# Windowed attention with a gated feed-forward: the RMS weight row by one broadcast transfer, its constant moved, first-block copies in halves, loads in a new order

## The chip, the cores and the metric

The kernel runs on one core of one Trainium2 chip. The core has a matrix engine (TensorE, PE in the profile, with its weight loads as PEld), a vector engine (VectorE, DVE), a scalar engine (ScalarE, ACT), a general engine (GpSimd, POOL), and a synchronising engine (SyncE, SP). SP, ACT and POOL issue DMA transfers. Each engine works through its own queue in order, and an instruction waits for its inputs by semaphores. The metric is the time of one execution on the device, in microseconds (us); lower is better.

## What is computed

Attention over a window of 128 positions and four sink positions, and a normalised gated feed-forward network on the result:

```python
# q, k, v: (4, 8, 768, 64) float32; n_sink 4, window 128
scores = q @ k^T / 8
keep = (pos_k < 4) | (0 <= pos_q - pos_k < 128)
a = softmax(where(keep, scores, -1e9)); x = a @ v        # -> (3072, 512)

rms = sqrt(mean(x * x, axis=-1) + 1e-06)
xn = x / rms * rms_g
g = xn @ w_gate                                         # (512, 1536)
silu = g / (1 + exp(-g))
out = (silu * (xn @ w_val)) @ w_out                     # (1536, 512)
```

## The kernel before

The 3072 tokens are 24 blocks of 128 (four batches of six blocks). For each block `g` the kernel loads q, k and v, transposes q and k (blocks 0 to 7 on PE with a copy out of PSUM, later ones by DMA), multiplies k by q of its own and the next block (`scores`, L445), takes the exponential on ACT (`exps`, L463), masks, and multiplies by v (`av`, L501). v has an extra column of ones for each head, so that the last column of the product is the denominator. On DVE `normal` (L526) divides by it. `square` (L537, on ACT) sums the squares of a row; `rms` (L545, on DVE) makes the reciprocal root by an integer first guess and a few small steps, and multiplies the block by it and by the weight row `gb`, into `xr`. `xr` is transposed on PE for blocks 0 to 8 (`pe_x`, L575), and copied out of PSUM (`copy_x`).

The feed-forward part works in groups `G` of four blocks. `ffn` (L832) does, for a set of 128-wide slices of the inner dimension (`fts`) and a set of columns, the gate matmuls (`g`), the value matmuls (`v`), the hyperbolic tangent on ACT (`tanh`), and two steps on DVE (`silu`, `hidden`). Group 0 is worked in four chunks of one block each (`CHUNKS`), four slices at a time, group 1 and 2 in two chunks. `project` multiplies by `w_out`, `evacuate` copies out, `store` writes.

The order of all of this is not written by hand. Every instruction is given to `Plan` (L27) with the engines that may run it, a duration, what it needs and gives, a priority and the PSUM banks that it takes and drops. `Plan.run` is a list scheduler: it repeatedly takes the operation that can start first, by its own durations, and the engines' queues are filled in that order. `Plan.land` says when it takes a transfer to be complete. So a changed duration, priority or load order can move instructions anywhere in the queues; at run time the queues are fixed and each instruction waits only for its real inputs.

Loads of q, k, v and the weights go through POOL's queue, float32 in memory to bfloat16 on chip, in the order of the string `LOADS`; at most `DEPTH` = 8 are outstanding. `w-0-2` stands for slices 0 and 1 of both `w_gate` and `w_val`. Block 0's k and q are loaded as float32 through SP (`F32_LOADS`) and cast on ACT. The weight row is loaded through SP as one row of 512 (`grow`, L341) between these two. `unit_gb` (L398) multiplies it by a column of ones in float32 on PE, which spreads it over the 128 partitions; `scale_gb` (L401, ACT) copies it out and multiplies it by `C3`, a constant of the reciprocal root.

The masks of blocks 0 and 1 are added before the scores by matmuls of a bias (`PE_MASKS` = 2, `mask_bias` L435, four matmuls for each block), those of blocks 2 to 15 are multiplications on DVE (`mask_dve` L475), and from block 16 on selections on POOL (`mask_pool`). The scores of blocks 0 and 1 are done in two parts (`SPLIT`), first for the block's own q and then for the next. `WARM` = 30 small matmuls on zeros fill gaps of PE early on.

```python
    LOADS = "q-1 k-1 v-0 w-0-2 v-1 qkv-2 qkv-3 w-2-4 w-4-6 w-6-8 w-8-9 w-9-12 qkv-4 wo-0-6 qkv-5 wo-6-12 qkv-6 qkv-8 qkv-7"
```

Of the kernel before, what the change touches and what calls it, by code (L numbers as in the profile page):

```python
# [9 lines left out]
ALU = mybir.AluOpType  # L10
# [5 lines left out]
P = 128  # L16
# [3 lines left out]
C3 = -5.0 / 16.0  # L20
# [6 lines left out]
class Plan:  # L27
# [5 lines left out]
    LATE = 300  # L33
    HOP = {"PE": 40, "ACT": 35, "DVE": 35, "POOL": 90, "SP": 60}
    START = {"PE": 800, "ACT": 800, "DVE": 1030, "POOL": 1290, "SP": 800}

    def __init__(self):
        self.ops, self.held = [], {}
        self.rings = {"POOL": 0, "HW": 0, "TR": 0}
        self.banks = {i: 0 for i in range(8)}  # L40
# [7 lines left out]

    def land(self, ring, first, work):


        r = self.rings
        if ring == "POOL":
            begin = max(first, r["POOL"], r["HW"])
            r["POOL"] = begin + (1.4 * work if begin < 8500 else work)
            self.loads -= 1
            return r["POOL"] + 520
        if ring == "HW":
            begin = max(first, r["HW"])
            r["HW"] = begin + (1.25 * work if begin > 2500 else work)  # L60
# [6 lines left out]
        return r["TR"] + (350 if ring == "TR" else 650)  # L67

    def run(self):
        free, users = dict(self.START), {}  # L70
        self.loads = sum(o["ring"] == "POOL" for o in self.ops)
# [10 lines left out]
        while left:  # L82
            first = None
            for e, found in cand.items():
                for o in found:
# [3 lines left out]
                    ready = o["ready"] + self.HOP[e] if o["ready"] else 0  # L89
                    if k:  # L90
                        ready = max(ready, sorted(self.banks.values())[k - 1] + 40)
                    start = max(free[e], ready)
                    key = (start, o["prio"], ready, o["at"])
# [6 lines left out]
            (start, *_), e, o = first  # L100
            for x in o["ways"]:
                cand[x].remove(o)
# [34 lines left out]
def kernel(  # L137
# [35 lines left out]
    CAST_DVE = 600  # L173
    MASKS_PRIO = -5
    POOL_AT = (1,2)
    DEPTH = 8
    LOADS = "q-1 k-1 v-0 w-0-2 v-1 qkv-2 qkv-3 w-2-4 w-4-6 w-6-8 w-8-9 w-9-12 qkv-4 wo-0-6 qkv-5 wo-6-12 qkv-6 qkv-8 qkv-7"
    LOADS += "".join(f" qkv-{g}" for g in range(9, NB))
    PE_MASKS = 2
    POOL_MASK_FROM = 16  # L180
# [3 lines left out]
    GATE_FROM = 6  # L184
    LOAD_LEAD = 9
    LEAD_FROM = 10
    WARM = 30
    GATE_LEAD = 6
    T_LEAD = 3
    SPLIT = (0,1)  # L190
    CHUNKS = (4,2,2)
    GB_PRIO = 2000
# [33 lines left out]
    ones = const.tile([1, P], FP32, name="ones")  # L226
    sel = const.tile([P, P], BF16, name="sel")
    headm = const.tile([P, H], FP32, name="headm")
    grow = const.tile([1, DM], FP32, name="grow")
# [22 lines left out]
    for b in range(B):  # L252
        dve(60, lambda b=b: nc.vector.memset(V16[b][:, :, :, D:VW], 1.0),
            gives=[("vone", b)], prio=-97 + b if b == 0 else -50)
    dve(150, lambda: nc.vector.memset(ones, 1.0), gives=["ones"], prio=-96)
# [77 lines left out]
    for i, name in enumerate(F32_LOADS):  # L333
# [8 lines left out]
        out=grow, in_=moe_rms_g.rearrange("(o d) -> o d", o=1)))}, (), ["grow"], -89.5,  # L342
        ring="HW", work=50)
    act(1290, None, (), ["table"], -80)

    issue = []
# [51 lines left out]
    def unit_gb():  # L398
# [520 lines left out]
```

The softmax here doesn't subtract the row's maximum and nothing guards it: scores larger than these inputs give would overflow.

## Time and profile before

| | |
|---|---|
| median of 8 runs | 247.02 us (246.54 to 247.48) |
| the profiled execution, own time | 246.54 us |
| its span, first to last instruction | 244.8 us |
| first feed-forward matmul starts | 20.16 us |
| PE / DVE / ACT / POOL busy | 234.1 / 183.3 / 131.1 / 88.7 us |
| PE matmuls recorded | 2098 |
| granted TensorE clock | 1.00 |

The profile is of one execution. Its page has busy times, the span in 40 slices, the chain of work that ended last, and the costliest groups of instructions; the trace behind it can be asked for the instructions of a stretch in order of time (the timeline), for busy times by stretch (the windows), and for who waited for whom. In a timeline line the first two numbers are the start and the duration in us, then come the engine, the line of the kernel, the operation, its tiles as output<-inputs, the shapes and the number of instructions that are drawn together; in brackets stands the idle time of the engine before it and what ended it. A line of the waits has what waited, for what, the sum in us, how often, and the longest.

### The profile page before, as it was taken

The page shows a single profiled execution, that of the slowest core. Times are in us where ns is not written, and L with a number is a line of the kernel's source. Part 1 is how long each engine was busy: PE and PEld are TensorE (multiplying, and loading weights), DVE is VectorE, ACT ScalarE, POOL GpSimd, SP SyncE. Part 2 cuts the span into 40 slices and gives each one's busy share as a digit, 9 for nine tenths or more (in the row PEclk, how much of TensorE's full clock was granted, in tenths as well). Part 3 has the DMA queues.
Part 4 walks back from the last instruction along what each step waited for, and adds up shares of the span by engine and source line. Part 5 has one row for each costly group of instructions (what it writes and reads, how often), then busy time and mean ns, then how long its engine had stood idle before and what let it go on. Part 6 is the DMA issues. An engine that isn't in the chain of part 4 may idle for free.

```text
span 244.8 us, 5510 instructions
## 1 busy us (share of the span) xinstructions
PE 234.1 (96%) x2098; PEld 148.8 (61%) x2120; DVE 183.3 (75%) x482; ACT 131.1 (54%) x276; POOL 88.7 (36%) x114
## 2 busy tenths in 40 slices
PE   4898999999999999999999999999999999999994
PEld 2477997776789775688874544444545544444443
DVE  4188979979899998899889499991299992377700
ACT  3577565778676647555627555735735521333111
POOL 8986755785354759522003300311604100000000
PEclk9999999999999999999999999999999999999999
DMA  8999999999999999999913644014311013200022
GB/s 109 173 168 196 192 188 188 155 130 174 158 202 142 155 127 168 163 209 147 157 15 89 151 107 86 3 21 102 114 45 21 4 21 107 86 3 0 0 86 86
DMA packets 111979, 27.22 MB, mean 111 GB/s; under 512 B 102097, under 2 KB 109009, under 8 KB 111954
## 3 DMA queue, kind: packets, MB, share of 16 engines
q0 software_dynamic: 80704, 13.90, 76.5%
q1 hardware_dynamic: 31106, 12.85, 27.4%
q8 instruction: 16, 0.26, 0.5%
q10 hardware_dynamic: 144, 0.13, 0.2%
q14 instruction: 9, 0.07, 0.1%
HBM read 28.31 MB, written 6.29 MB: 141 GB/s over the span
## 4 chain that ended last, share of the span: by engine, by line
PE 81%; DVE 10%; issue 3%; ACT 2%; DMA 2%; SPq 0%; DVEq 0%; ACTq 0%
PE o L790 22%; PE v L757 22%; PE g L757 21%; PE s L456 4%; PE av L520 2%; DVE hT L780 2%; DMA stage<-in_q_dram 2%; DVE p L770 2%; DVE r L560 2%; PE av L515 2%; DVE xr L564 2%; PE av L505 1%; ACT e L469 1%; PE o_last L808 1%; DVE x L532 1%
## 5 line engine op out<-in xcount | busy, mean ns | idle before, releaser
L757 PE MATMUL v<-xnt,wv 128*128 128x128 bf16 (+2 forms) x522 | 71.0, 281 | 0.3
L757 PE MATMUL g<-xnt,wg 128*128 128x128 bf16 (+2 forms) x525 | 69.5, 282 | 0.1
L764 ACT ACTIVATE th<-g 128x512 bf16<-128x512 f32 x72 | 42.9, 600 | 45.4 <-PE g L757 41.3
L790 PE MATMUL o<-wo,hT 128*128 128x512 bf16 x263 | 62.6, 379 | 1.2 <-issue 0.6
L770 DVE SCALAR_TENSOR_TENSOR p<-th,g 128x512 bf16<-128x512 bf16 x72 | 48.0, 681 | 15.7 <-ACT th L764 15.2
L757 PEld LDWEIGHTS <-wg 128*128 128x128 bf16 x528 | 43.1, 98 | 19.1 <-issue 0.6
L757 PEld LDWEIGHTS <-wv 128*128 128x128 bf16 x528 | 42.7, 98 | 18.4 <-issue 0.8
L469 ACT ACTIVATE e<-s 128x512 bf16<-128x512 f32 (+1 forms) x104 | 48.2, 540 | 7.6 <-PE s L456 7.4
L780 DVE TENSOR_TENSOR hT<-p,v 128x512 bf16<-128x512 bf16 x72 | 47.2, 680 | 1.5 <-PE v L757 0.6
L790 PEld LDWEIGHTS <-hT 128*128 128x128 bf16 x276 | 25.6, 98 | 28.6 <-issue 1.3
L491 POOL TENSOR_SCALAR_AFFINE_SELECT e<-e 128x512 bf16<-128x512 bf16 x14 | 9.4, 680 | 64.4 <-ACT e L469 51.4
L798 ACT ACTIVATE osb<-o 128x512 f32<-128x512 f32 x23 | 13.8, 598 | 29.1 <-PE o L790 29.1
L323 POOL DMA_DIRECT2D k<-in_k_dram x23 | 20.4, 886 | 16.2 <-DMA v<-in_v_dram 7.2
L323 POOL DMA_DIRECT2D q<-in_q_dram x23 | 20.5, 892 | 13.5 <-DMA k<-in_k_dram 7.2
L327 POOL DMA_DIRECT2D v<-in_v_dram x24 | 21.3, 887 | 7.9 <-DMA q<-in_q_dram 4.4
L532 DVE TENSOR_TENSOR x<-av,rden 128x256 bf16<-128x256 f32 x48 | 20.4, 424 | 1.6
L531 DVE RECIPROCAL rden<-av 128x4 f32<-128x4 f32 x48 | 8.4, 175 | 16.5 <-PE av L520 16.5
L540 ACT ACTIVATE sq<-x 128x512 bf16<-128x512 bf16 x24 | 15.1, 631 | 9.7 <-DVE x L532 9.6
L564 DVE SCALAR_TENSOR_TENSOR xr<-x,r,gb 128x512 bf16<-128x512 bf16 x24 | 19.0, 790 | 0.9
L486 DVE TENSOR_TENSOR e<-e,masks 128x1024 bf16<-128x1024 bf16 (+1 forms) x30 | 18.9, 649 | 0.9 <-ACT e L469 0.8
L520 PE MATMUL av<-v,e 128*128 128x65 bf16 x192 | 17.2, 195 | 0.3 <-ACT e L469 0.3
L456 PE MATMUL s<-qkT 64*128 64x256 bf16 (+1 forms) x208 | 14.6, 262 | 0.6 <-ACT qkT L423 0.6
(70 smaller groups left out, 180.7 us busy)
## 6 DMA issues: line engine op xcount, KB each, us to landing
out_dram<-osb SPq DMA_DIRECT2D x23, 256.0 KB, 2.2
v<-in_v_dram POOLq DMA_DIRECT2D x24, 128.0 KB, 10.6
q<-in_q_dram POOLq DMA_DIRECT2D x23, 128.0 KB, 10.8
k<-in_k_dram POOLq DMA_DIRECT2D x23, 128.0 KB, 10.5
wo<-in_moe_w_out_dram POOLq DMA_DIRECT2D x2, 768.0 KB, 11.9
wg<-in_moe_w_gate_dram POOLq DMA_DIRECT2D x4, 256.0 KB, 7.5
wv<-in_moe_w_val_dram POOLq DMA_DIRECT2D x4, 256.0 KB, 7.8
wg<-in_moe_w_gate_dram POOLq DMA_DIRECT2D x1, 384.0 KB, 10.3
```

The lines of the kernel that those rows point to most:

```text
L323: nc.gpsimd.dma_start(out=T[name, g], in_=block_of(src, g))
L327: nc.gpsimd.dma_start(out=V16[b][:, t, :, 0:D], in_=block_of(v, g))
L456: nc.tensor.matmul(out=BANK[slot][:, j * 256 + n0 * P:j * 256 + n1 * P], lhsT=qkT[pr, 1, hp, t * P:(t + 1) * P], rhs=qkT[pr, 0, hp, (t + n ...
L469: nc.scalar.activation(out=T["e", g, u][:, 2 * hi:2 * hi + 2, n0:n1, :].rearrange("p x n c -> p x (n c)"), in_=ps.rearrange("p (j c) -> p ...
L520: nc.tensor.matmul(out=dest, lhsT=T["e", g, u][:, x, 0, :], rhs=V16[b][:, t, h, :], start=(t == 0), stop=True, skip_group_check=True,)
L532: nc.vector.tensor_tensor(out=T["x16", g][:, 4 * u:4 * u + 4, :], in0=pvv[:, :, 0:D], in1=rden.unsqueeze(2).to_broadcast((P, 4, D)), op=AL ...
L564: nc.vector.scalar_tensor_tensor(out=T["xr", g], in0=T.pop(("x16", g)).rearrange("p h d -> p (h d)"), scalar=r[:, 3:4], in1=gb, op0=ALU.mu ...
L757: nc.tensor.matmul(out=ps[:, i * n:(i + 1) * n], lhsT=w_sb[:, kt, ft * P:(ft + 1) * P], rhs=T["xnt", G][:, kt, cols], start=(kt == 0), sto ...
L764: nc.scalar.activation(out=T["th", key], in_=BANK[("g", key)], func=ACT.Tanh, scale=0.5,)
L770: nc.vector.scalar_tensor_tensor(out=T["p1", key], in0=T.pop(("th", key)), scalar=1.0, in1=BANK.pop(("g", key)), op0=ALU.add, op1=ALU.mult,)
L780: nc.vector.tensor_tensor(out=T[hk][:, i:i + n, cols], in0=T.pop(("p1", key)).rearrange("p (n c) -> p n c", n=n), in1=BANK.pop(("v", key)) ...
L790: nc.tensor.matmul(out=BANK[("o", G, tb)], lhsT=T["h", G, ft // 4][:, ft % 4, tb * P:(tb + 1) * P], rhs=wo[:, ft, :], start=(ft == 0), sto ...
```

## The change

The weight row is loaded straight into the 128 rows of `gb`, by one transfer that repeats the row, issued on SP behind both block 0 loads. The float32 matmul, the scaling on ACT, the column of ones and the row tile are gone. The constant `C3` is gone too: the mean square is scaled by `GAIN` and its small summand by the same, and the extra column of v is -1 instead of 1, for the sign.

For blocks 0 to 2 (`SQD` = 3) the sum of squares is made on DVE by one multiply with a sum, in place of ACT's square and DVE's addition. Block 0 (`HALVES`, `XHALVES` = 1) has its q and k copies done in halves, one on ACT and one on DVE, and its multiplication by the weight row, its transposes and the copies behind them in two halves.

Block 1 is masked on DVE instead of by matmuls, and its scores are done in one part. Blocks 12 to 15 get their masks on POOL where POOL did it from 16 on. The first chunk of group 0 takes two slices at a time (`FIRST` = 2), with half-size tiles. Sink values wait for the first block's `xr` in the plan. There are 20 warm-up matmuls. The loads come in a new order: both v of blocks 0 and 1 and blocks 2 and 3 ahead of all weights, weight slices 2 to 8 ahead of 0 and 1, and slices in smaller pieces. The plan's model of the DMA queues, some due times (`LATER`, `MARGIN`, `T_LEAD`, `GATE_FROM`) and its choice among operations that could start are changed.

```diff
-C3 = -5.0 / 16.0
+GAIN = (16.0 / 5.0) ** 2
+EPS = 1e-6 * GAIN
...
     def land(self, ring, first, work):
...
-            begin = max(first, r["POOL"], r["HW"])
-            r["POOL"] = begin + (1.4 * work if begin < 8500 else work)
+            begin = max(first, r["POOL"])
+            if begin > 17500 and not self.fetched:
+                begin, self.fetched = begin + 900, True
+            r["POOL"] = self.end(begin, work, ((self.hard, 0.34), (6000, 0.7)))
...
-            r["HW"] = begin + (1.25 * work if begin > 2500 else work)
+            r["HW"] = self.end(begin, work, ((3500, 1.05), (1e9, 0.4)))
...
-        return r["TR"] + (350 if ring == "TR" else 650)
+        return r["TR"] + (350 if ring == "TR" else 650) + self.LATER
...
-    CAST_DVE = 600
+    CAST_DVE = 800
-    POOL_AT = (1,2)
+    POOL_AT = (1,1)
-    LOADS = "q-1 k-1 v-0 w-0-2 v-1 qkv-2 qkv-3 w-2-4 w-4-6 w-6-8 w-8-9 w-9-12 qkv-4 wo-0-6 qkv-5 wo-6-12 qkv-6 qkv-8 qkv-7"
+    LOADS = "q-1 k-1 v-0 v-1 qkv-2 qkv-3 w-2-4 w-4-5 w-5-6 w-6-9 w-0-1 w-1-2 w-9-10 w-10-11 qkv-4 w-11-12 wo-0-6 qkv-5 wo-6-12 qkv-8 qkv-7 qkv-6"
-    PE_MASKS = 2
-    POOL_MASK_FROM = 16
+    PE_MASKS = 1
+    POOL_MASK_FROM = 12
-    GATE_FROM = 6
+    GATE_FROM = 7
-    WARM = 30
+    WARM = 20
-    T_LEAD = 3
-    SPLIT = (0,1)
+    T_LEAD = 4
+    SPLIT = (0,)
+    FIRST = 2
+    SQD = 3
+    HALVES = 1
+    XHALVES = 1
...
-        dve(60, lambda b=b: nc.vector.memset(V16[b][:, :, :, D:VW], 1.0),
+        dve(60, lambda b=b: nc.vector.memset(V16[b][:, :, :, D:VW], -1.0),
...
-        out=grow, in_=moe_rms_g.rearrange("(o d) -> o d", o=1)))}, (), ["grow"], -89.5,
-        ring="HW", work=50)
+        out=gb, in_=moe_rms_g.rearrange("(o d) -> o d", o=1).to_broadcast((P, DM))))},
+        (), ["gb"], -70, ring="HW", work=660)
...
-    def unit_gb():
-        nc.tensor.matmul(out=bank(("gb",)), lhsT=ones, rhs=grow, start=True, stop=True)
-
-    def scale_gb():
-        nc.scalar.mul(gb, BANK.pop(("gb",)), C3)
...
+        if g < SQD:
+            x16 = T["x16", g].rearrange("p h d -> p (h d)")
+            sq = xpool.tile([P, DM], BF16, name="sq")
+            nc.vector.tensor_tensor_reduce(
+                out=sq, in0=x16, in1=x16, scale=GAIN / DM, scalar=EPS, op0=ALU.mult,
+                op1=ALU.add, accum_out=m,
+            )
...
+    def scale_x(g, cols):
+        if ("xr", g) not in T:
+            T["xr", g] = xpool.tile([P, DM], BF16, name="xr")
         nc.vector.scalar_tensor_tensor(
-            out=T["xr", g], in0=T.pop(("x16", g)).rearrange("p h d -> p (h d)"),
-            scalar=r[:, 3:4], in1=gb, op0=ALU.mult, op1=ALU.mult,
+            out=T["xr", g][:, cols], in0=T["x16", g].rearrange("p h d -> p (h d)")[:, cols],
+            scalar=T["r", g], in1=gb[:, cols], op0=ALU.mult, op1=ALU.mult,
         )
...
+            k = min(nc_, FIRST) if G == 0 and c == 0 else nc_
+            for ft in range(0, FTN, k):
+                ffn(G, n, range(ft, ft + k), slice(c * w, (c + 1) * w), p0 + 10 * n)
```

## The prediction

> **What bounds the kernel now.** I read the busy table first, then windows, the chain, the waits of TensorE (PE), and the timeline of the start. PE is busy 96% of the span, but a pipelined matmul counts as busy while it waits for a slot, so the windows matter more:
>
> ```profile
> PE 234.1 (96%) x2098; PEld 148.8 (61%) x2120; DVE 183.3 (75%) x482; ACT 131.1 (54%) x276; POOL 88.7 (36%) x114
> ...
> 10.00:15.00 5.00, 5.00 (x30) 2.24 (x30) 2.13 (x9) 3.15 (x10) 4.93 (x7) 1.00 2.33 158
> 15.00:20.00 5.00, 4.15 (x78) 3.19 (x77) 4.36 (x17) 4.29 (x13) 4.10 (x6) 1.00 1.72 185
> 20.00:25.00 5.00, 4.57 (x86) 4.37 (x87) 4.68 (x14) 3.28 (x8) 2.74 (x4) 1.00 1.49 195
> 25.00:30.00 5.00, 5.00 (x93) 5.00 (x91) 4.59 (x13) 2.63 (x6) 3.52 (x5) 1.00 1.47 197
> 30.00:40.00 10.00, 10.00 (x185) 9.64 (x182) 8.59 (x16) 5.54 (x10) 5.71 (x7) 1.00 1.82 183
> ```
>
> The columns are busy us (and instruction counts) of PE, weight loads, VectorE (DVE), ScalarE (ACT), GpSimd (POOL), then the granted clock, DMA share, GB/s. From 10 to 15 PE runs 30 matmuls, from 25 on 18 to 19 a microsecond. So the kernel has a start of some 20 us, in which PE is mostly waiting, and a dense body. Between 15 and 30 DVE is busy 13.6 of 15 us: it is the tight engine there. The waits of PE and the timeline say what ends the start:
>
> ```profile
> PE s L438 <- DVE bias L273: 2.1, 1, 2.1
> PE q L416 <- ACT q L319: 1.1, 1, 1.1
> ...
> PE o L790 <- issue: 0.6, 4, 0.2
> PE s L456 <- ACT qkT L423: 0.6, 1, 0.6
> PE x L579 <- DVE xr L564: 0.4, 1, 0.4
> ```
>
> ```profile
> 6.92 0.62 ACT L319 CAST q<-stage 128x512 bf16<-128x512 f32 x1 [2.39 <-DMA stage<-in_q_dram]
> ...
> 9.63 2.07 PE L399 MATMUL gb<-grow,ones 1*128 1x512 f32 x2
> ...
> 12.61 0.18 DVE L531 RECIPROCAL rden<-av 128x4 f32<-128x4 f32 x1 [3.10 <-PE av L520]
> ```
>
> ```profile
> 20.16 1.06 PE L757 MATMUL g<-xnt,wg 128*128 128x128 bf16 x16
> ...
> 21.64 0.40 PE L579 MATMUL x<-ident,xr 128*128 128x128 bf16 x4 [0.43 <-DVE xr L564]
> ...
> 27.16 0.75 DVE L564 SCALAR_TENSOR_TENSOR xr<-x,r,gb 128x512 bf16<-128x512 bf16 x1
> ...
> 28.00 0.39 PE L579 MATMUL x<-ident,xr 128*128 128x128 bf16 x4
> ```
>
> The fp32 matmul that spreads the weight row holds PE for 2.07 us while block 0's exponentials are ready. The feed-forward part begins at 20.16, block 1 is transposed at 21.64 after a wait for DVE, block 2 at 28.00 without one. After that PE's only listed wait is 0.6 us. So the end of the kernel is set by when PE gets past the last early wait, plus the PE work left from there. I compare the two kernels by that sum at one place, block 2's transpose (call it X2).
>
> **The change, part by part.**
>
> PE work. Gone are the two-pass fp32 matmul (2.0 us), block 1's mask matmuls (4 of 216 ns warm, 0.86) and ten warm-up matmuls (0.56); block 1's scores in one part save 0.4 and leave its share of the early queue shorter. All of it stands before the feed-forward part, where PE waits anyway, so its removal counts only through what follows. What is left behind the first feed-forward matmul is the same work in both orders. But the order up to X2 differs. Before: seven groups of 16 matmuls (0.89 each, from the chain's rows such as x16 in 0.89), one transpose group (0.22) and block 2's AV (0.69), 7.14 us. After: six groups of 8 and two of 16, that is five times 0.89, plus the same 0.91, 5.36 us. So when the changed kernel reaches X2 it has 1.79 us more PE work in front of it than the old one.
>
> When is X2 in the changed kernel? The q stage load is issued at 1.33 instead of 1.83, since the weight row goes behind it on SP (nothing else stands on SP's queue until block 8's transposes). It took 5.1 us, the k one ahead of it 3.1; the hardware queue moved 535 packets from 2.5 to 3.0 but 249 from 3.0 to 3.5, a gap that the earlier issue closes. Landing between 4.4 and 6.4, I take 5.2 (6.89 before). Cast 0.62, transposes 0.63 behind PE's masks, halved copies (bounds 0.30, a quarter of the four 128x256 exponentials' 1.21, and 0.42, DVE's 128x256 row): q is ready at 7.3. PE's queue has block 1's q transposes next; that load landed at 7.1 and now shares the DMA with 256 KB of weight row: 6.5 to 7.9, I take 7.1. Scores at 7.6 (9.09 before), a 0.59 copy first on ACT, exponentials from 8.5, AV at 9.5 without the fp32 matmul, first reciprocal at 9.95 (bounds 9.3 and 10.7) against 12.61: 2.66 us earlier. The DVE then is the chain. Its instructions from that reciprocal to block 2's weight multiply, by the order of its queue: three normalisations at 1.19 (12.61 to 13.80); three squares with sum, now on DVE, not in the trace, between 0.68 (the 128x512 multiply of L770) and 0.98 (0.79 of xr and 0.19 for a reading of the sum as ACT has it), 0.80 taken; three Newton chains at 0.90 (26.26 to 27.16); the weight multiply of block 0 in halves, 2 times 0.49 (0.75 less 256 elements at 1.04 ns), of blocks 1 and 2 at 0.75; masks of blocks 1 and 2, 2.56 (block 2's took 1.28); sink keys 0.79, sink values 0.80, one copy 0.42, three half-size feed-forward steps at 0.42. Sum 3.57 + 2.40 + 2.70 + 0.98 + 1.50 + 2.56 + 0.79 + 0.80 + 0.42 + 1.26 = 16.98 us, against 15.30 in the old trace (12.61 to 27.91, with its waits for ACT). With 0.5 us for waits (block 3's load, AV of block 2; bounds 0 and 1.0) the multiply ends at 27.4 and X2 is at 27.5, only 0.5 earlier than 28.00. So: 0.5 gained, 1.79 more left, net **1.3 us later**. Block 0 reaches PE about 3 us earlier (near 17.2), but PE then waits for DVE with block 1 and block 2; the stall moves from 14 to 20 us to 18 to 27 us.
>
> The loads say the same. w-0-2 is moved from the fourth place to behind w-6-9, past seven block loads and the weights 2 to 8 on POOL's queue; the bias selection goes ahead of the k load, which is issued 0.4 later. Block 3's v landed at 18.0; without w-0-2 in front (9.0 to 11.5) it comes 2.5 us earlier, with the weight row later by between nothing and 1.3 us (256 KB at 195 GB/s), less 0.4 of the closed gap: 15.65 taken. Then 17 pieces of 128 KB until the gate weights 0 to 1 are there, at 0.665 (18.0 to 31.3 us for 20 pieces): 26.95. The group that needs them stands directly behind X2. So even an infinitely fast DVE leaves X2 worth about 26.7 (25.9 to 27.6), a gain of 1.3 against 1.79 given back.
>
> What costs nothing: the row's landing on DVE's queue (block 0's first half multiply waits for it, block 1's masks are behind) has cover, as it is issued at 1.83 and needed at about 14; even with the 5.1 us of the q stage behind another 5.1 it is there at 12. The constant moved into the square's scale and the -1 columns change no instruction count.
>
> Later. Masks of blocks 13 to 15 go from DVE to POOL: six multiplies at 0.68, 4.1 us, leave a DVE that is busy 8.8 to 9.3 of 10 us there; twelve selections of 0.64 come onto POOL, whose waits are hidden as long as AV follows late enough. More cautious due times for transposes may close some of PE's small late stalls. There is little to win: 0.6 us in the waits. I take 0.4 gained, bounds 1.0 gained and 0.5 lost.
>
> Sum: 1.3 - 0.4 = 0.9 later. On the profiled execution, 246.54 (span 244.8 and 1.7 around it), that is 247.4; the median of the runs is 0.48 above it, so **247.9**.
>
> A rule of the Trainium skill speaks against the change. The trace first: eight scores took 0.61 at 11.63 and 0.40 at 15.00, after PE had been busy 5.00 of 5.00 us from 10 to 15. "TensorE: Matmul & The Clock Gate", in the section on why this matters, says that about 4 us of unbroken activity are needed for the full rate and that gaps of some 3 us lose it. That page has PE, which now has fewer fillers and a gap of 3 us from 18.2 to 21.5, at half rate until about 25. By the trace alone the sum stays 247.9; by the rule AV of block 2 would take some 0.4 us more and X2 with it, 248.3.
>
> **The rivals.**
>
> 1. The lead reaches the body (faster). Loads land early and the square is cheap: reciprocal at 9.3, squares at 0.68, no waits: 9.3 + 16.6 = 25.9, X2 at 26.0, 2.0 gained less 1.79, 0.2, with the later 1.0 gained in all 1.2, so 245.8. For it: DVE's idle 3.1 us before the first reciprocal is really filled, and 2.0 us of fp32 matmul are really gone. Against: the weights' place, 26.95, must move too, to 26.1 or earlier.
> 2. No change to see. X2 at 26.8 and the later gain of 0.4 cancel within 0.3: 247.0 to 247.2. Both halves are small, so this is close to the forecast.
> 3. PE stays at its slow rate through 25 us, or the weight row delays the block loads by its full 1.3 us: AV of block 2 late, DVE waits 1.0, reciprocal at 10.7: X2 at 29.0, 1.0 lost and 1.79, less 0.4: 2.4 later, 249.4. For it: half as many PE instructions from 10 to 20. Against: PE has slack before X2.
> 4. The start doesn't get earlier at all (q lands at 6.4 as a 5.1 us load): part of 3, X2 at 28.4, 248.8.
>
> **How the numbers follow.** Forecast 0.50 (its own range 247.3 to 248.7), rival 1 0.24, rival 2 0.14, rivals 3 and 4 0.12. A difference under 0.2% (0.5 us) can't be told from none. Faster: rival 1 and a little of 2, 0.25. Within: most of 2 and the lower edge of the forecast, 0.19. Slower: 0.56. The range reaches into rival 1 and to rival 3: 245.5 to 249.4.
>
> **What would show it.** Right: the q stage landing near 5.2, the first reciprocal near 10, the first feed-forward matmul near 17, then PE waiting on xr near 21 and 27, and DVE without idle time from 10 to 27. Wrong at the loads: first reciprocal outside 9.3 to 10.7. Wrong at DVE: block 2's xr ending before 26.2, or its idle time above 1 us. Wrong at the weights: block 2's transpose followed by a wait for wg. If X2 is at 27.5 and the time is still shorter than before, the later masks and due times are worth more than 1.0.

## The result, and the profile after

The changed kernel takes 250.53 us (median, 248.29 to 255.39); the kernel before, run beside it, 246.86. The ratio is 1.0093, 95% interval 1.0077 to 1.0109: 2.3 us later, where 0.9 was forecast. Executions more than 1.5% above a kernel's fastest are left out of the ratio; five of this kernel's twelve were ("The masks" comes back to them), and the other seven have a median of 249.15. The profiled execution took 250.6 us, 1.45 above that median; its span is 248.5, 3.7 more than before. So the profile below accounts for 3.7 us, where the ratio says 2.3.

From the page of the changed kernel, the busy table and the granted clock in 40 slices:

```profile
PE 234.0 (94%) x2076; PEld 148.3 (60%) x2096; DVE 182.0 (73%) x486; ACT 128.5 (52%) x272; POOL 100.1 (40%) x132
...
PEclk9998899999999999999999999999999999999999
```

PE is as busy as before in a longer span. The windows of its start (PE, weight loads, DVE, ACT, POOL, granted clock, DMA share, GB/s):

```profile
10.00:15.00 5.00, 4.44 (x54) 2.80 (x50) 2.96 (x12) 4.08 (x12) 4.27 (x6) 1.00 2.31 154
15.00:20.00 5.00, 4.14 (x60) 2.91 (x58) 4.73 (x15) 5.00 (x13) 3.88 (x6) 1.00 1.67 188
20.00:25.00 5.00, 2.67 (x37) 2.36 (x35) 4.59 (x15) 1.45 (x4) 3.83 (x6) 0.79 1.44 194
25.00:30.00 5.00, 5.00 (x80) 5.00 (x79) 3.41 (x14) 0.87 (x2) 3.77 (x5) 0.87 1.82 179
```

PE is less busy than before from 20 to 25 us (2.67 of 5, before 4.57), and its granted clock falls to 0.79. The timeline of the changed kernel gives the places by which the forecast counted:

```profile
6.67 0.62 ACT L351 CAST q<-stage 128x512 bf16<-128x512 f32 x1 [1.91 <-DMA stage<-in_q_dram]
...
9.31 0.61 PE L440 MATMUL q<-ident,q 128*128 128x128 bf16 x4 [1.25 <-DMA q<-in_q_dram]
...
12.22 0.18 DVE L558 RECIPROCAL rden<-av 128x4 f32<-128x4 f32 x1 [0.75 <-PE av L547]
...
19.00 0.61 PE L863 MATMUL g<-xnt,wg 128*128 128x128 bf16 x8
...
22.54 0.40 PE L635 MATMUL x<-ident,xr 128*128 128x128 bf16 x4 [2.33 <-DVE xr L620]
...
27.54 0.75 DVE L620 SCALAR_TENSOR_TENSOR xr<-x,r,gb 128x512 bf16<-128x512 bf16 x1
...
28.66 0.39 PE L635 MATMUL x<-ident,xr 128*128 128x128 bf16 x4
```

Block 1's q is transposed at 9.31 behind a wait for its load, the first reciprocal comes at 12.22 instead of the 9.95 forecast, and block 2's transposes (X2) stand at 28.66, later than the old 28.00. The waits of PE:

```profile
PE x L635 <- DVE xr L620: 2.3, 1, 2.3
PE q L440 <- DMA q<-in_q_dram: 2.3, 4, 1.3
PE s L466 <- DVE bias L305: 1.9, 1, 1.9
...
PE o L902 <- DMA wo<-in_moe_w_out_dram: 0.3, 1, 0.3
```

PE now waits for loads, which it did nowhere on the old list. Two numbers follow the loss through the kernel. The first is the time of a place plus the PE work left behind it (all matmuls still to come, at the spacings of the warm ones in the old trace); where it grows, PE lost time. The second is the moment at which POOL can issue again behind the first half of `w_out`, which shows how far the stream of loads has got, since in both orders the same loads stand ahead of it.

| kernel | first reciprocal | X2 | sum at X2 | sum at block 8 | place behind w_out | ratio |
|---|---|---|---|---|---|---|
| before | 12.61 | 28.00 | 236.3 | 237.9 | 37.84 | 1 |
| changed | 12.22 | 28.66 | 238.8 | 242.2 | 41.26 | 1.0093 |
| row_narrow | 9.31 | 26.22 | 236.3 | 240.0 | 39.58 | 1.0224 |
| old_with_broadcast | 12.44 | 29.98 | 237.4 | 239.6 | 39.44 | 1.0066 |
| old_spread_later | 11.84 | 27.26 | 235.6 | 237.8 | 38.77 | 0.9957 |
| old_spread_later_q_first | 10.25 | 27.06 | 235.4 | 237.6 | 38.09 | 0.9993 |
| gap_filled | 11.62 | 28.42 | 238.5 | 242.7 | 40.88 | 1.0184 |
| masks_on_dve_same_order | 12.13 | 28.63 | 238.7 | 242.1 | 41.97 | 1.0117 |
| row_late_masks_dve | 9.29 | 27.99 | 238.1 | 241.2 | 40.93 | 1.0127 |
| row_narrow_masks_dve_filled | 9.37 | 25.93 | 236.0 | 240.8 | 39.06 | 1.0096 |
| weights_halved | 12.07 | 29.37 | 239.5 | 241.3 | 37.13 | 1.0044 |
| row_narrow_masks_dve_filled_weights_halved | 10.07 | 25.96 | 236.1 | 237.8 | 36.88 | 0.9980 |

Up to X2 the changed kernel loses 2.45 us: 0.66 of time and the 1.79 of work that its order leaves for later. From X2 to block 8 it loses 3.5, the old one 1.6: another 1.9. From there to the last matmul it needs 0.7 less (2.86 against 3.52). Together that is the 3.7 us of the spans. Which of these parts is smaller in the executions nearer to the median is not shown, as only this one was profiled.

### The profile page after: what moved, and what is told of

Same layout as the page of the kernel before. It is cut to its first block, busy times and chain, and to the rows that moved or that the text cites. A ratio compares the mean times of both kernels' runs of the same rounds, so it can differ in the third digit from the quotient of the medians.

```text
span 248.5 us, 5496 instructions
## 1 busy us (share of the span) xinstructions
PE 234.0 (94%) x2076; PEld 148.3 (60%) x2096; DVE 182.0 (73%) x486; ACT 128.5 (52%) x272; POOL 100.1 (40%) x132
## 4 chain that ended last, share of the span: by engine, by line
PE 77%; DMA 12%; POOL 6%; DVE 3%; issue 2%; POOLq 0%
PE o L902 22%; PE g L863 22%; PE v L863 21%; DMA wo<-in_moe_w_out_dram 5%; PE s L483 4%; DMA wv<-in_moe_w_val_dram 4%; DMA v<-in_v_dram 3%; PE av L547 2%; PE av L542 2%; POOL wv L402 1%; PE av L532 1%; POOL wg L402 1%; PE o_last L920 1%; POOL v L359 1%; POOL q L355 1%
## 5 line engine op out<-in xcount | busy, mean ns | idle before, releaser
L863 PE MATMUL g<-xnt,wg 128*128 128x128 bf16 (+2 forms) x521 | 71.0, 283 | 0.5
L881 DVE SCALAR_TENSOR_TENSOR p<-th,g 128x512 bf16<-128x512 bf16 (+1 forms) x75 | 48.7, 661 | 21.8 <-ACT th L874 21.3
L874 ACT ACTIVATE th<-g 128x512 bf16<-128x512 f32 (+1 forms) x75 | 42.9, 584 | 39.8 <-PE g L863 39.3
L863 PEld LDWEIGHTS <-wv 128*128 128x128 bf16 x528 | 43.6, 99 | 18.7 <-issue 0.2
L891 DVE TENSOR_TENSOR hT<-p,v 128x512 bf16<-128x512 bf16 (+1 forms) x75 | 47.8, 659 | 1.2 <-PE v L863 0.5
L518 POOL TENSOR_SCALAR_AFFINE_SELECT e<-e 128x512 bf16<-128x512 bf16 x20 | 13.3, 668 | 66.0 <-ACT e L496 46.6
L355 POOL DMA_DIRECT2D k<-in_k_dram x23 | 20.5, 892 | 11.3 <-DMA v<-in_v_dram 6.6
L577 ACT ACTIVATE sq<-x 128x512 bf16<-128x512 bf16 x21 | 13.2, 629 | 18.8 <-DVE x L559 18.8
L620 DVE SCALAR_TENSOR_TENSOR xr<-x,r,gb 128x512 bf16<-128x512 bf16 (+1 forms) x25 | 18.6, 743 | 0.9
L547 PE MATMUL av<-v,e 128*128 128x65 bf16 x192 | 17.8, 198 | 0.0
L513 DVE TENSOR_TENSOR e<-e,masks 128x1024 bf16<-128x1024 bf16 (+1 forms) x26 | 16.1, 643 | 0.8 <-ACT e L496 0.6
L542 PE MATMUL av<-v,e 128*128 128x65 bf16 x160 | 15.3, 196 | 0.1
```

The source lines that it names most:

```text
L355: nc.gpsimd.dma_start(out=T[name, g], in_=block_of(src, g))
L542: nc.tensor.matmul(out=dest, lhsT=T["e", g - 1, u][:, x, 1, :], rhs=V16[b][:, t - 1, h, :], start=(t == 1), stop=False, skip_group_check=True,
L547: nc.tensor.matmul(out=dest, lhsT=T["e", g, u][:, x, 0, :], rhs=V16[b][:, t, h, :], start=(t == 0), stop=True, skip_group_check=True,)
L620: nc.vector.scalar_tensor_tensor(out=T["xr", g][:, cols], in0=T["x16", g].rearrange("p h d -> p (h d)")[:, cols], scalar=T["r", g], in1=gb ...
L863: nc.tensor.matmul(out=ps[:, i * n:(i + 1) * n], lhsT=w_sb[:, kt, ft * P:(ft + 1) * P], rhs=T["xnt", G][:, kt, cols], start=(kt == 0), sto ...
L874: nc.scalar.activation(out=T["th", key], in_=BANK[("g", key)][:, 0:n], func=ACT.Tanh, scale=0.5,)
```

## The experiments

### The weight row

Four kernels ask what the row's transfer costs. `row_narrow` and `row_twice` keep every queue's order and change the transfer alone; `old_with_broadcast` and `old_spread_later` give the kernel before one part each: the broadcast row (with `GAIN` in place of `C3`, as in the changed kernel), or its own fp32 matmul put behind block 0's AV. In these two `Plan` orders PE, DVE and ACT anew, so their times are those of the part and of a new order together.

```diff
 # row_narrow
-        out=gb, in_=moe_rms_g.rearrange("(o d) -> o d", o=1).to_broadcast((P, DM))))},
+        out=gb[:, 0:32], in_=moe_rms_g.rearrange("(o d) -> o d", o=1)[:, 0:32].to_broadcast((P, 32))))},
 # row_twice
+        for t in (gb, gb2):
+            nc.sync.dma_start(
+                out=t, in_=moe_rms_g.rearrange("(o d) -> o d", o=1).to_broadcast((P, DM)))
 # old_with_broadcast
-        out=grow, in_=moe_rms_g.rearrange("(o d) -> o d", o=1)))}, (), ["grow"], -89.5,
+        out=gb, in_=moe_rms_g.rearrange("(o d) -> o d", o=1).to_broadcast((P, DM))))},
+        (), ["gb"], -70, ring="HW", work=660)
-    pe(1000, unit_gb, ["ones", "grow"], ["gbm"], GB_PRIO, takes=[("gb",)], mode=2)
-    act(490, scale_gb, ["gbm", "table"], ["gb"], drops=[("gb",)])
 # old_spread_later
-    pe(1000, unit_gb, ["ones", "grow"], ["gbm"], GB_PRIO, takes=[("gb",)], mode=2)
+    pe(2000, unit_gb, ["ones", "grow", ("av", 0, 1)], ["gbm"], -1000, takes=[("gb",)])
```

> Leaves out most of the weight row: 32 of its 512 columns are loaded, the others are set to 1. Every queue keeps its order. Theory A (the row's transfer takes the DMA from the block loads: block 1's q was in use at 9.31 instead of 7.59 us, the q stage landed at 6.67): block 1's q transposes start at 7.6 or before, the first reciprocal at 10.0 to 10.6 instead of 12.22, block 2's transpose at 27.0 instead of 28.66, time 1.5 to 2.5 us below the changed kernel's, 246.8 to 247.8. Theory B (the order of VectorE's queue and the PE work left behind block 2 decide, the row does not): block 2's transpose not before 28.3, time within 0.6 us of the changed kernel's 249.2 (before times the ratio 1.0093).

> The row is transferred twice, the second time to a tile that nobody reads; all queues keep their order. Theory A: the block loads are late by another 1.5 to 3 us, first reciprocal at 13.5 to 15, time 1.5 to 3 us above the changed kernel's, 250.7 to 252.2. Theory B: within 0.6 us of the changed kernel's 249.2.

> The old kernel with the one part alone: the row by a broadcast transfer behind both stage loads, the constant in the scale, no fp32 matmul. Theory A: block loads 1.5 to 2.5 us late, the fp32 matmul's 2.0 us gained, time 0 to 2 us above the old one, 246.9 to 248.9. Theory B: only the matmul's 2.0 us on PE are gone, first reciprocal at 10.6 to 11.3 instead of 12.61, time 0.8 to 1.5 us below the old one, 245.4 to 246.1.

> The old kernel with the fp32 matmul behind block 0's AV in the plan instead of between the two parts of the scores; no broadcast transfer. If the matmul's place was what held block 0 (AV at 12.17 us with exponentials done at 10.73), the first reciprocal comes at 11.2 to 11.6 instead of 12.61 and the time falls by 0.5 to 1.2 us, to 245.7 to 246.4. If the weights and VectorE set the place of block 2's transpose anyway, it stays within 0.4 us of 246.9.

Measured: `row_narrow` 252.47 us, ratio 1.0224 (1.0205 to 1.0243); `row_twice` 255.45, 1.0253 (1.0227 to 1.0279), with two executions at 252.99 and 253.59 and two at 257.31 and 257.41; `old_with_broadcast` 248.72, 1.0066 (1.0049 to 1.0084); `old_spread_later` 245.95, 0.9957 (0.9941 to 0.9973), faster than both kernels.

What the row does is in the DMA view from 4 to 7 us (queue, kind: packets, MB, share of 16 engines; then for a load issued in this time its KB and the us until it landed). The changed kernel:

```profile
q0 software_dynamic: 1268, 0.16, 83.7%
q1 hardware_dynamic: 392, 0.29, 35.1%
...
q<-in_q_dram POOLq DMA_DIRECT2D x1, 128.0 KB, 7.5
```

and `row_narrow`:

```profile
q0 software_dynamic: 2681, 0.34, 177.0%
q1 hardware_dynamic: 319, 0.06, 14.3%
...
q<-in_q_dram POOLq DMA_DIRECT2D x1, 128.0 KB, 4.6
```

Beside the row, POOL's queue (q0, the block loads) moved 0.16 MB in these 3 us instead of 0.34, and a q load issued then took 7.5 us instead of 4.6. The row's packets are the large ones of q1: from 5 to 6 and from 6 to 7 us it started 72 and 70 packets, 42 and 55 of them of 2 KB, and they took 64 and 76 ns on the mean, where the q1 packets of `row_narrow` in 5 to 6 us took 18. From 2 to 10 us q0 moved 0.58 MB instead of 0.78, and both queues together 1.36 instead of 1.31: the loads lost most of what the row took. At the 0.15 MB per us that q0 has from 9 to 10 us these 0.20 MB are 1.3 us. But the first twelve loads land 2.2 to 3.1 us later than in `row_narrow` (block 3's v at 17.2 instead of 14.8); why they lag by more than the bytes is not shown. The timeline of `row_narrow`:

```profile
6.78 0.39 PE L441 MATMUL q<-ident,q 128*128 128x128 bf16 x4
...
9.31 0.18 DVE L559 RECIPROCAL rden<-av 128x4 f32<-128x4 f32 x1 [0.57 <-PE av L548]
...
26.22 0.39 PE L636 MATMUL x<-ident,xr 128*128 128x128 bf16 x4
```

Block 1's q is ready 2.5 us earlier than with the full row (9.31), the first reciprocal 2.9, X2 2.4. With two rows the same places are at 10.15, 13.06 and 29.82: 0.84 more for the first reciprocal, less than the 1.5 to 3 us that were expected. In `old_with_broadcast` the first reciprocal is at 12.44 and X2 at 29.98, and without any fp32 matmul the kernel is 1.6 us slower; how much of this is the new order's is not shown (PE waits 1.6 us there for `xnt`, which it does nowhere on the old list). `row_narrow` has the early start that was expected of it and not the time. It is 2.1 us behind the kernel before at block 8 (240.0 against 237.9), and later PE loses 2.6 at one place, in its waits and in the timeline of POOL at 109 us:

```profile
PE av L548 <- POOL e L519: 2.6, 1, 2.6
```

```profile
109.64 0.87 POOL L360 DMA_DIRECT2D v<-in_v_dram  x1 [3.00 <-DVE hT L892]
110.52 0.65 POOL L519 TENSOR_SCALAR_AFFINE_SELECT e<-e 128x512 bf16<-128x512 bf16 x1
```

A mask of block 13 stands on POOL's queue behind a load that waits 3.00 us, and PE waits 2.6 for the mask.

The old kernel's own spread, only put later, needs 1.12 us where it took 2.07 at 9.63, and is not in front of block 0's exponentials any more (timeline of `old_spread_later`):

```profile
11.84 0.18 DVE L531 RECIPROCAL rden<-av 128x4 f32<-128x4 f32 x1 [0.20 <-PE av L520]
...
13.40 1.12 PE L399 MATMUL gb<-grow,ones 1*128 1x512 f32 x2
...
27.26 0.39 PE L579 MATMUL x<-ident,xr 128*128 128x128 bf16 x4
```

`old_spread_later_q_first` also moves its one-row load behind the q stage (`GROW` at -70 instead of -89.5).

> The old kernel with the fp32 matmul behind block 0's AV (old_spread_later: 245.95) and the one-row load behind the q stage load instead of before it. The q stage should land near 5.3 instead of 7.0, the first reciprocal at 10.4 to 11.0 instead of 11.84, and the time fall by another 0.5 to 1.3 us, to 244.7 to 245.5. If the weights and VectorE now hold block 2's transpose: within 0.4 us of 245.95.

246.49 us, 0.9993 (0.9976 to 1.0010). The first reciprocal is 2.4 us earlier than before and X2 0.9, and the time is the same, where 244.7 to 245.5 was expected: in this order, again a new one, the earlier start is worth nothing measurable.

### The masks

```diff
 # masks_from_16
-    POOL_MASK_FROM = 12
+    POOL_MASK_FROM = 16
 # masks_on_dve_same_order
     def mask_pool(g, u, n):
+        if g < 16:
+            nc.vector.tensor_tensor(
+                out=et, in0=et, in1=masks[:, 1, n:n + 1, :].to_broadcast((P, 4, P)), op=ALU.mult)
+            return
```

> The changed kernel with one part undone: the masks of blocks 12 to 15 on VectorE again. With the narrow row PE waited 2.6 us for block 13's mask, which stood on GpSimd's queue behind a v load that waited 3.0 us. Theory C (this wait comes and goes with the loads and makes the changed kernel's runs spread from 248.3 to 255.4): the runs agree within 1 us, at 248.0 to 249.6, and PE waits for GpSimd nowhere. Rival (the move is harmless, the spread is from the start): the spread stays over 3 us.

> The changed kernel with the masks of blocks 13 to 15 emitted on DVE at the places that the plan gave them on POOL; every other queue keeps its order. Nothing is left out. Theory 1 (the masks behind loads on POOL's queue cost time in some executions only): the start is that of the changed kernel (first reciprocal 12.0 to 12.4, block 2's transpose 28.5 to 28.8), no wait of PE's for a mask on POOL, the times of the runs lie within 1 us of each other, 248.3 to 249.6, ratio 1.006 to 1.010. Theory 2 (those masks cost nothing): same spread as the changed kernel, 248.3 to 255, and the same ratio 1.009.

`masks_from_16`, replanned: 249.36 us (248.62 to 249.90), 1.0090 (1.0057 to 1.0124). `masks_on_dve_same_order`: 249.68 (248.53 to 250.72), 1.0117 (1.0070 to 1.0163). Their runs spread over 1.3 and 2.2 us, more than the 1 us expected of each, and in the first PE still waits 0.7 us for a mask on POOL. But none of these nine runs is above 250.72, while five of the changed kernel's twelve lie between 252.6 and 255.4. Those five are 3.5 to 6.2 us above the median of the other seven, 249.15. So the masks on POOL probably cost some executions that much and the others little; without them the ratio is no better, so the loss in it is elsewhere. None of the five was profiled, but one execution of `row_twice` was that took 257.41, 3.8 us or more above that kernel's two shorter ones, and it has such a wait:

```profile
PE av L551 <- POOL e L522: 4.2, 1, 4.2
```

All four runs of `row_narrow`, which has one too, lie at 252.4 to 252.9. The masks alone don't do it: `weights_halved` below keeps them on POOL, and its twelve runs lie between 247.07 and 249.39.

### Parts of the change undone in a replanned kernel

Six kernels have the spread on PE behind block 0's AV in place of the broadcast, and `POOL_MASK_FROM` = 16. They undo further parts: the square on ACT again (`SQD` = 0, in all but the first), the old `LOADS`, the old due times (`LATER`, `MARGIN` = 0, `T_LEAD` = 3, `GATE_FROM` = 6), `FIRST` = 4, or block 1's masks on PE with its scores in two parts.

```diff
+    pe(2000, unit_gb, ["ones", "grow", ("av", 0, 1)], ["gbm"], -1000, takes=[("gb",)])
+    act(490, lambda: nc.scalar.copy(gb, BANK.pop(("gb",))), ["gbm", "table"], ["gb"], -30,
+        drops=[("gb",)])
...
-    SQD = 3
+    SQD = 0
```

> As masks_from_16, and the row is spread by the old fp32 matmul on PE, placed behind block 0's AV, instead of by the broadcast transfer. Theory A: block 1's q transposes start before 7.0, first reciprocal at 9.2 to 9.8, block 2's transpose at 26.0 to 27.2, time 1.5 to 2.5 us below masks_from_16: 246.0 to 247.6. If the row's transfer were not the cause: within 0.6 us of masks_from_16.

> As pe_row_masks_16, with the squares of blocks 0 to 2 on ScalarE again. Theory B (VectorE is the chain between first reciprocal and block 2's transpose): three times 0.77 us leave VectorE, three trips to ScalarE of 0.8 come in where it would wait; block 2's transpose moves by 0.5 to 1.5 us earlier and the time with it if the weights are there. Rival (the trips cost as much as they save): within 0.4 us of pe_row_masks_16.

> pe_row_masks_16_act_square (248.45) with the old order of the loads. In it and in the changed kernel PE lost 0.9 us between the transposes of blocks 2 and 3 against 0.4 in the old kernel, with waits for wg and wv of 0.5 each. Theory D (the new load order brings the weights that PE works on next too late and leaves 1.8 us more PE work behind block 2's transpose): with the old order PE waits under 0.3 us for weights, 1 to 1.8 us less PE work are left there, time 0.8 to 1.6 us less, 246.9 to 247.7. Rival E (the due times of the transposes and gates cost it later): within 0.5 us of 248.45.

> pe_row_masks_16_act_square (248.45) with the old due times: nothing added to the landing of transposes, no margin on PE, lead 3, gate from block 6. Theory E: 0.5 to 1.2 us less, 247.2 to 248.0. Theory D: within 0.4 us of 248.45.

> As act_square_old_loads, and the first chunk takes four slices at a time as in the old kernel. Theory D: no further gain, within 0.4 us of act_square_old_loads. Rival (the half-size pieces cost VectorE and ScalarE their fixed time): 0.4 to 1 us less.

> pe_row_masks_16_act_square (248.45) with block 1's masks on PE and its scores in two parts again. Theory B (VectorE is the chain up to block 2's transpose): 1.28 us leave VectorE, block 2's transpose comes 0.5 to 1.2 us earlier than 26.15, and the time falls by as much unless the weights hold the place just behind it (theory D: time within 0.4 us of 248.45 though the transpose's input is earlier).

| kernel | us | ratio | first reciprocal | place behind w_out |
|---|---|---|---|---|
| pe_row_masks_16 | 249.84 | 1.0113 (1.0079 to 1.0146) | 9.73 | 39.64 |
| pe_row_masks_16_act_square | 248.45 | 1.0073 (1.0049 to 1.0097) | 10.02 | 38.91 |
| act_square_old_loads | 249.34 | 1.0096 (1.0065 to 1.0126) | 9.37 | 37.98 |
| act_square_old_due_times | 249.75 | 1.0116 (1.0087 to 1.0144) | 9.66 | 39.20 |
| act_square_old_loads_whole_chunk | 251.69 | 1.0195 (1.0150 to 1.0240) | 9.53 | 37.84 |
| act_square_pe_masks | 249.00 | 1.0101 (1.0052 to 1.0151) | 9.81 | 39.57 |

All have the early first reciprocal that the change was forecast to give, and all are slower than before; X2 lies anywhere from 26.15 to 30.80. No single part undone wins it back, but the six can't be read further: each gets a new order on all engines, and the intervals overlap. With the old loads the stream is where it was (37.98), and the granted clock is down to 0.63 from 10 to 15 us, where PE waits 2.3 us for block 2's q. So the later experiments hold every queue's order and change one transfer or one engine.

### PE's gap

```diff
         ps = bank(("x", g)).bitcast(BF16)
+        for _ in range(30 if g == 1 else 0):
+            nc.tensor.matmul(out=BANK["x", g][:, 0:P], lhsT=zeros, rhs=zeros, start=True, stop=True)
```

> The changed kernel with 30 small matmuls on zeros placed in PE's queue just ahead of block 1's transposes, where PE stood idle for 2.33 us; nothing else moves. Nothing of the computation is left out. Both theories: the granted clock, 0.79 from 20 to 25 us and 0.87 from 25 to 30 us, goes to 1.00, and block 2's AV takes 0.35 us a group instead of 0.67. Theory 1 (DVE's chain sets block 2's transpose, the clock loss lies beside it): DVE was busy from 22.4 to 28.3 us, so block 2's transpose moves only from 28.66 to 28.3 to 28.5, and the time falls by 0.2 to 0.4 us, ratio to before 1.007 to 1.009. Theory 2 (the clock loss is on the path): PE spent 6.1 us from block 1's transpose to block 2's for 4.5 us of work, so block 2's transpose comes near 27.2 and the time falls by 1.2 to 1.6 us, ratio 1.003 to 1.005.

250.76 us, 1.0184 (1.0129 to 1.0238): not the small gain that was expected but more than the changed kernel's 1.0093, with intervals that do not meet. The window and X2 of this kernel:

```profile
20.00:25.00 5.00, 3.98 (x77) 3.79 (x75) 4.68 (x15) 1.27 (x4) 3.24 (x5) 1.00 1.45 194
```

```profile
28.42 0.40 PE L637 MATMUL x<-ident,xr 128*128 128x128 bf16 x4 [0.54 <-DVE xr L620]
```

The clock is 1.00 from 20 to 30 us, and now X2 waits for DVE: 0.24 us earlier, no more. The lower clock lay beside DVE's chain. Theory 1 holds at X2 and fails in the time. In its profile, of an execution of 251.01, PE waits 1.6 us for a k load at 56.76, and the sum at block 8 is 242.7, 0.5 above the changed kernel's. That this is the whole of the difference is not shown.

### The stream of loads

Four kernels with every queue's order held (the last two add two memsets on DVE before 7 us). The first has the narrow row, the masks on DVE and the gap filled, all as above. The second has the full row, issued only behind block 3's q load. The other two leave out half of the rows of weight slices 2 to 8.

```diff
 # row_late_masks_dve
+            if n == 7:
+                nc.gpsimd.memset(gb[:, 0:1], 0.0)
+                nc.sync.dma_start(
+                    out=gb, in_=moe_rms_g.rearrange("(o d) -> o d", o=1).to_broadcast((P, DM)))
 # weights_halved, row_narrow_masks_dve_filled_weights_halved
+            kts = slice(0, KTN // 2 if 2 <= f0 < 9 else KTN)
-                out=w_sb[:, :, cols], in_=src[:, :, cols]),
+                out=w_sb[:, kts, cols], in_=src[:, kts, cols]),
```

> The changed kernel with the weight row's load cut to 32 of 512 columns (the rest is set to 1), the masks of blocks 13 to 15 on DVE in the same order, and PE's gap ahead of block 1's transposes filled. Left out: the weights of 480 columns. Theory 1 (the row's transfer, the POOL masks and the later waits of PE for q, k and w_out are the whole loss): block 1's q at 6.8, first reciprocal 9.3, block 2's transpose 25.6 to 26.0, no wait for a mask on POOL; the start is worth what the old one was (time plus work left 236.0 to 236.3 there), and only the later waits remain, 0.7 to 1.5 us: 247.6 to 248.4, ratio 1.003 to 1.006. Theory 2 (the replanned start is worth its lead once its faults are mended): 245.5 to 246.5, ratio under 0.999. Theory 3 (something else later costs the same as the POOL wait did): 250 or more.

> The changed kernel with its full weight row issued on SP only after POOL has issued the q load of block 3, and the masks of blocks 13 to 15 on DVE in the same order. Nothing is left out. Theory 1 (it is the row's place beside the block loads that costs): block 1's q lands as with the narrow row, its transposes at 6.7 to 7.0, first reciprocal 9.2 to 9.7; the row lands at 11 to 14, where block 0's weight multiply may wait up to 1 us for it; block 2's transpose 26.2 to 27.3; time 247.8 to 249.2, ratio 1.004 to 1.009, faster than with the masks alone moved. Theory 2 (the row costs the same wherever it stands): the later loads are 2 us late instead, block 2's transpose 28 or later, and the time is that of the kernel with the masks alone moved.

`row_narrow_masks_dve_filled`: 249.45 us, 1.0096 (1.0059 to 1.0132). None of its three theories gave the time. The start came as forecast (X2 25.93, the sum there 236.0), and yet 4.8 us are lost from there to block 8, where the kernel before loses 1.6. PE's timeline shows by what in part:

```profile
17.75 0.62 PE L870 MATMUL v<-xnt,wv 128*128 128x128 bf16 x8 [0.85 <-DMA wv<-in_moe_w_val_dram]
22.64 1.51 PE L870 MATMUL g<-xnt,wg 128*128 128x128 bf16 x24 [0.72 <-DMA wg<-in_moe_w_gate_dram]
24.58 1.51 PE L870 MATMUL v<-xnt,wv 128*128 128x128 bf16 x24 [0.43 <-DMA wv<-in_moe_w_val_dram]
27.22 1.29 PE L870 MATMUL g<-xnt,wg 128*128 128x128 bf16 x20 [0.69 <-DMA wg<-in_moe_w_gate_dram]
...
54.90 0.40 PE L441 MATMUL k<-ident,k 128*128 128x128 bf16 x4 [1.56 <-DMA k<-in_k_dram]
```

Each of these is a wait for a transfer. The first three come before X2 and are in its sum already; the last two and one of 0.25 at 31.89 are 2.5 of the 4.8 us.

`row_late_masks_dve`: 249.72, 1.0127 (1.0095 to 1.0159). The first reciprocal is at 9.29, then DVE waits for the row:

```profile
14.70 0.48 DVE L631 SCALAR_TENSOR_TENSOR xr<-x,r,gb 128x256 bf16<-128x256 bf16 x1 [2.13 <-DMA gb<-in_moe_rms_g_dram]
```

It was issued at 9.20 and took 5.4 us. X2 is at 27.99, the place behind `w_out` at 40.93, and the time is that of `masks_on_dve_same_order` within the intervals: in the time, this other place of the row beside loads gained nothing. It is no clean comparison of the start, as PE now waits 2.6 us for block 3's q and has a granted clock of 0.50 from 15 to 20 us.

> The changed kernel with only the first half of the contraction rows of weight slices 2 to 8 loaded (the rest is set to zero on DVE in its idle time before 7 us); every queue keeps its order. Left out: half of the rows of w_gate and w_val for seven slices of twelve, 0.9 MB of the load stream. Theory 1 (DVE sets block 2's transpose, the load stream costs the waits behind it): first reciprocal about 12.2 and block 2's transpose 28.3 to 28.8 as in the changed kernel, the place on POOL's queue behind w_out's first half comes at 36 to 38 instead of 41.3 us, PE waits for no load from 28 to 60, time 248.4 to 249.4, ratio 1.006 to 1.010. Theory 2 (the order, not the loads): the waits of PE behind 28 us stay and the time is that of the changed kernel, 250 or more.

> As the kernel with the narrow row, masks on DVE and the gap filled, and with half of the rows of weight slices 2 to 8 not loaded; every queue keeps its order. Left out: 480 of the 512 columns of the weight row and half of the rows of w_gate and w_val for seven slices. Theory 1 (the early start runs into the load stream): the waits for wv and wg at 17.8, 22.6, 24.6 and 27.2 go, block 2's transpose is at 25.2 to 26.0, and what was lost between there and 60 us (4.8 us of time plus work left) falls to under 2: time 246.0 to 247.0, ratio 0.995 to 1.001. Theory 2 (the planned order, not the loads): the lead is lost in any case, 248.7 to 249.6, ratio 1.007 to 1.011.

`weights_halved`: 247.80 us, 1.0044 (1.0030 to 1.0058). The start is no earlier (X2 even 29.37), no load is waited for between 28 and 60 us, and the loss from X2 to block 8 falls from 3.5 to 1.8. The other one: 246.18, 0.9980 (0.9969 to 0.9992), where the same kernel with whole weights had 1.0096. Its X2, and POOL's place behind `w_out`:

```profile
25.96 0.40 PE L645 MATMUL x<-ident,xr 128*128 128x128 bf16 x4 [0.84 <-DVE xr L628]
```

```profile
36.88 0.88 POOL L358 DMA_DIRECT2D q<-in_q_dram  x1 [2.97 <-DMA wo<-in_moe_w_out_dram]
```

The same place in the kernel before, and in the changed one:

```profile
37.84 0.87 POOL L323 DMA_DIRECT2D q<-in_q_dram  x1 [2.56 <-DMA wo<-in_moe_w_out_dram]
```

```profile
41.26 0.88 POOL L355 DMA_DIRECT2D q<-in_q_dram  x1 [2.82 <-DMA wo<-in_moe_w_out_dram]
```

X2 is where it was with whole weights; the sum now grows by 1.7 to block 8 instead of 4.8, and 3 us come back in the time. Theory 1 holds in both; in the first it gave more than it said (1.0044 against 1.006 to 1.010). So the planned order by itself doesn't hold the start back: it runs into the stream of loads, which is 3.4 us late in the changed kernel. The kernel before was not run with halved weights. But it has no wait for a load on its list, and its sum grows by 1.6 from X2 to block 8, as that of the two kernels with halved weights does (1.8 and 1.7).

## Why the prediction was wrong

The direction and the skeleton held; the size failed at one term in the start and one later. In the forecast's sum, X2 was to be 0.5 us earlier, 1.79 us of work were to be left over, and 0.4 were to be gained later: 0.9. In the profiled execution X2 is 0.66 later, the 1.79 are there, and 1.25 are lost later: 3.7.

- "With the weight row later by between nothing and 1.3 us", and block 1's q "6.5 to 7.9, I take 7.1": this is the step that failed in the start. With the row, block 1's q is in use at 9.31 instead of 6.78, and block 3's v lands 2.4 us later (17.2 against 14.8, where 15.65 was taken). Its price was taken from its bytes at the rate of the body, 1.3 us, and that is about what POOL's queue lost in bytes; but engines wait for whole loads to land, and these came 2.2 to 3.1 us later. With the narrow row the first reciprocal is at 9.31, inside the forecast's 9.3 to 10.7. So the row is shown to be what holds the start back. In the time it is not: with the masks on DVE in both, the narrow row and the filled gap give 249.45 against 249.68, within the intervals, as long as the weights are loaded whole. Rival 3 had this mechanism with 1.3 us and 249.4.
- The q stage "5.2": 6.67 in this profile, 5.28 to 5.40 in three others with the same row and order (`gap_filled`, `masks_on_dve_same_order`, `weights_halved`), whose first reciprocal is at 11.6 to 12.1 all the same. It is not what sets the start; block 1's q is.
- DVE's chain, 16.98 and 0.5 for waits: 16.07 measured from the first reciprocal to the end of block 2's multiply. The durations add up to 16.55, neighbours overlap by 0.48 in their starts and ends, and there is no wait. Square with sum took 0.69 and 0.08, against 0.80. Without these 1.4 us the late start would have cost that much more.
- "1.79 more PE work in front of it": 210.09 us left behind X2 against 208.30. This was right, and the runs show it: with the narrow row X2 is 1.8 us earlier than in the kernel before, and the sum there is the same 236.3. The whole lead of the start goes into the order.
- The weights for the group behind X2, "26.95": this had the right mechanism, and the row's price in it was too small. In the changed kernel the load of these gate weights is issued at 20.55 and lands 8.0 later, at 28.55, outside the 25.9 to 27.6 of the forecast; the 17 pieces behind block 3's v took 11.3 us, as forecast. The group behind X2 begins at 28.88, so a faster DVE could have brought it forward by little. With the narrow row that group waits until 27.10 and 27.22. The term says that the loads bound the start, however early DVE is, and should have carried more weight.
- "Later": 0.4 gained, bounds 1.0 gained and 0.5 lost. Measured 1.9 lost between X2 and block 8 and 0.7 gained behind it, 1.25 lost in all; in size this term failed most. The step looked for late gains in masks and due times and didn't carry the stream's delay past X2: with the weights halved the sum grows by 1.8 to block 8 instead of 3.5, though the waits for loads that the changed kernel's profile lists there are only 0.7 us. Of the stream's 3.4 us at 41 us the row accounts for 1.7 (39.58 with the narrow one) or 2.9 (41.97 against 39.06, with the masks on DVE). That the rest is the new load order with its smaller pieces is argued, not shown; the old order took 0.93 off in a replanned kernel (38.91 against 37.98), and nothing separated order from pieces.
- "Whose waits are hidden as long as AV follows late enough": not in every execution; the masks on POOL cost 2.6 us at one place of `row_narrow`'s profile.
- The rule of the Trainium skill, "TensorE: Matmul & The Clock Gate", section on why this matters, is that gaps of some 3 us lose the rate. Here a shorter one was enough: 2.33 us idle before 22.54, and a granted clock of 0.79 and 0.87 in the two windows there. The forecast's price for it, 0.4 us at X2, is near the 0.24 that filling the gap gave.

Of the rivals, 4 named what happened to the start (it doesn't get earlier, 248.8) with the q stage as its cause, and 3 the cause. Its 249.4 is what the ratio makes of the 247.02 before (249.3), and that is luck in part: it has 1.0 lost at X2 and 0.4 gained later, where the profile has 0.66 and 1.25 lost. Rival 1, the lead that reaches the body, would need loads that come earlier: with the narrow row X2 is 2.4 us earlier, and with the masks on DVE and the gap filled 4.8 us are lost behind it, 2.5 of them in waits for loads.

What stays open: why none of the six replanned kernels beats the one before, what lengthens the time of `gap_filled`, and what the new load order adds to the stream's delay. A load order that keeps the old pieces with every queue else held was not tried.

## What to carry to other kernels

Where loads run without a break through the start of a kernel, engines that are ready earlier gain little: work out first when the last load of each stage can land, and count a new transfer by when the ones beside it land, not by its bytes alone. Spreading a row by DMA isn't free because no engine is busy with it; here the one-row load and a matmul behind block 0's AV, in a newly planned order, took 0.9957 of the time before, and the broadcast row in another took 1.0066. And a selection on the queue that also issues loads can wait behind a load that waits for its buffer.

## What the runs showed of the hardware

- A 256 KB broadcast from one 2 KB row took 6.9 us from issue to landing beside block loads in the changed kernel, and 5.4 when it was issued at 9.20 (`row_late_masks_dve`). The software queue beside the first moved 0.16 MB in 3 us instead of 0.34.
- The same fp32 matmul of 1x512 in two passes took 2.07 us at 9.63 in the kernel before and 1.12 at 13.40 in `old_spread_later`. The windows show a granted clock of 1.00 for both, but the records of the clock in these traces begin at 14.42 and 12.21, so the 1.00 at 9.63 is not a measurement.
- After an idle time of 2.33 us of PE the granted clock was 0.79 from 20 to 25 us, and AV of 65 columns was spaced at 55 ns instead of 30; with the gap filled (`gap_filled`) the clock there was 1.00.
